# GpSimd in place of VectorE for the last decoding step of w_out, in the fused agent-attention and rational-MoE kernel

## The chip, the core and the metric

The kernel runs on one core of a Trainium2 chip. The core has five engines that run side by side and wait for each other through semaphores: TensorE (PE in the profile; its weight loads are PEld), VectorE (DVE), ScalarE (ACT), GpSimd (POOL) and SyncE (SP), which only issues DMAs here. GpSimd issues DMAs too, beside its arithmetic. The metric is the device time of one execution in microseconds (us).

## The reference

Agent attention in two stages, and after it a feed-forward layer with a rational activation. B is 2, N is 12480 tokens, the width is 128, there are 49 agents and 2048 hidden units.

```python
def sm(a, b):
    s = scale * (a @ b.transpose(0, 2, 1))
    s = s - s.max(-1, keepdims=True)
    e = np.exp(s)
    return e / (e.sum(-1, keepdims=True) + 1e-09)
agent_v = sm(agents, k) @ v
x = (sm(q, agents) @ agent_v).reshape(B * N, 128)

h = x @ w_in                                   # 24960 x 2048
P = a[0] + a[1] * h + a[2] * h**2 + a[3] * h**3
Q = 1.0 + np.abs(b[0]) * np.abs(h) + np.abs(b[1]) * h**2
out = (P / (Q + 1e-06)) @ w_out
```

w_in and w_out arrive as float64. The kernel turns them into float32 on the chip: that is the decoding of which the title speaks.

## The kernel before

The first 60 us are the setup: it makes scores and softmax of the agents over the keys of batch 0, decodes w_in, and decodes the first two of the four pieces of w_out (512 columns each, numbered 0 to 3). Then a branch on the value `flag` picks one of two main loops; with these inputs it is the fast one (`rest(True)`).

The main loop goes over 262 units. A unit is three chunks of 128 hidden units for a block of 512 tokens, so most of its tiles are 128 x 1536. For unit i:

- TensorE makes the hidden values in one of two PSUM slots (`mm1`, L495 and L496, six matmuls). It does so for unit i+1 in iteration i, and the slot is free when VectorE has finished with unit i-1.
- ScalarE squares them into the tile u (L560).
- VectorE makes the denominator part w from slot and u (L589), then the numerator part u from u and slot (L581).
- ScalarE takes logarithm and exponential of w, for two units at once (L574 and L576).
- A DMA that GpSimd issues adds a constant from the DRAM tile omd to u, for two units at once (`add_om`, L601). Before that, GpSimd builds the constant (L610), and SyncE writes it to omd (L611).
- Five iterations later GpSimd multiplies u by w (L643). Every sixteenth unit, and for the last seven, VectorE does this (L594); behind a sixteenth one GpSimd waits for it with a small copy (L646).
- Seven iterations later TensorE multiplies u by w_out into a PSUM bank (`mm2`, L503). In the first seven iterations there is nothing to multiply yet, and TensorE runs dummy matmuls (L657).

The order on each engine is the order of the program's text; no scheduler changes it. Within an iteration the calls stand as `act`, ScalarE's held work, `dve2`, `dve1`, VectorE's held work, `add_om`, L643, GpSimd's held work, and `mm1` of the next unit. "Held work" comes from three streams (queries, w_out, keys of batch 1), each of which puts a step into the lists `hold["ACT"]`, `hold["DVE"]`, `hold["POOL"]` per iteration.

Decoding a piece needs two copies on ScalarE (L177, L178), three bit operations on VectorE (L181 to L183), a multiply and an add on GpSimd (L186, L187) and at last one operation on VectorE that sets small numbers to zero (`end`, L190). In the fast loop each piece is also scaled by a factor that is known only at run time (`w_scale`, L680, on GpSimd).

Pieces 0 and 1 are decoded in the setup: the `end` of piece 0 stands behind the GpSimd steps of piece 1, and that of piece 1 is the last line of the setup. Both are scaled at the head of the main loop. Pieces 2 and 3 are decoded in the main loop by `w_stream`. Their temporaries lie in tiles of the main loop that are not in use yet: those of piece 2 in the u tiles of units 6 and 7, those of piece 3 (t, s, r, z, each 512 columns) side by side in the w tile of units 6 and 7. The `end` of piece 2 and its scaling are held for iteration 4, those of piece 3 for iteration 5. So the operation L589 of unit 6 writes over the columns in which piece 3 keeps r.

Of the kernel before, what the change touches and what calls it, by code (L numbers as in the profile page):

```python
# [16 lines left out]
ALU = mybir.AluOpType  # L17
# [28 lines left out]
TINY2 = float(np.uint32(0x38100000).view(np.float32)) ** 2  # L46
# [35 lines left out]
def agent_attention_rational_moe(  # L82
# [12 lines left out]
    PE, ACT, DVE, POOL, SP = nc.tensor, nc.scalar, nc.vector, nc.gpsimd, nc.sync  # L95
# [22 lines left out]
    wo = const.tile([128, NFC, 128], F32, name="wo")  # L118
# [15 lines left out]
    def ring(pool, n, shape, dt, nm):  # L134

        r = rings.setdefault((pool.name, nm), [[], 0])
        if len(r[0]) < n:
            r[0].append(pool.tile(shape, dt, name=f"{nm}_{len(r[0])}"))
        r[1] += 1
        return r[0][(r[1] - 1) % n]  # L140
# [26 lines left out]
    WP = DFF // 4  # L167

    def load_w(raw, src, h):
        SP.dma_start(out=raw, in_=src.bitcast(I32).rearrange("p (f w) -> p f w", w=2)[:, h * WP:(h + 1) * WP, :])  # L170

    def decode(raw, t, s, r, z, dst):

        lo, hi = raw[:, :, 0], raw[:, :, 1]

        def act():
            ACT.activation(out=r, in_=lo.bitcast(U32), func=AF.Copy, scale=2.0 ** -52)  # L177
            ACT.activation(out=z, in_=hi.bitcast(F32), func=AF.Square)  # L178

        def dve():  # L180
            DVE.tensor_scalar(out=t, in0=hi, scalar1=3, scalar2=0x3FFFFFFF, op0=ALU.logical_shift_left, op1=ALU.bitwise_and)  # L181
            DVE.scalar_tensor_tensor(out=t, in0=hi, scalar=-0x40000000, in1=t, op0=ALU.bitwise_and, op1=ALU.bitwise_or)
            DVE.tensor_scalar(out=s, in0=t, scalar1=-0x00800000, scalar2=None, op0=ALU.bitwise_and)  # L183

        def pool():
            POOL.tensor_tensor(out=r, in0=r, in1=s.bitcast(F32), op=ALU.mult)  # L186
            POOL.tensor_tensor(out=r, in0=r, in1=t.bitcast(F32), op=ALU.add)  # L187

        def end():
            DVE.scalar_tensor_tensor(out=dst, in0=z, scalar=TINY2, in1=r, op0=ALU.is_ge, op1=ALU.mult)  # L190

        return act, dve, pool, end
# [119 lines left out]
    co, arm, made = {}, {}, set()  # L312
# [365 lines left out]
    def w_scale(h):  # L678
        w = wo.rearrange("p a b -> p (a b)")[:, h * WP:(h + 1) * WP]
        POOL.tensor_scalar(out=w, in0=w, scalar1=co["Kg"], scalar2=1.0, op0=ALU.mult, op1=ALU.mult)  # L680

    def w_tiles(fast):

        u = [t[:, h].rearrange("p j t -> p (j t)") for t in rings["wk", "u"][0] for h in range(2)]
        w = [t.rearrange("p h j t -> p (h j t)") for t in rings["wk", "w"][0]]

        def part(t, i, n, dt):
            return t[:, i * WP:(i + n) * WP].bitcast(dt)

        raw = [part(t, i, 2, I32).rearrange("p (f w) -> p f w", w=2) for t, i in (((u[8], 0), (u[9], 0)) if fast else ((w[2], 0), (w[2], 2)))]  # L690
        second = [(w[3], i) for i in range(4)] if fast else [(u[8], 0), (u[8], 1), (u[9], 0), (u[9], 1)]
        tmp = [[part(t, i, 1, dt) for (t, i), dt in zip(ts, (I32, I32, F32, F32))]
               for ts in ([(u[6], 0), (u[6], 1), (u[7], 0), (u[7], 1)], second)]
        return raw, tmp

    def w_stream(fast):
        raw, tmp = w_tiles(fast)
        for h in range(2):
            load_w(raw[h], w_out, h + 2)
        decs = [decode(raw[h], *tmp[h], wo.rearrange("p a b -> p (a b)")[:, (h + 2) * WP:(h + 3) * WP]) for h in range(2)]  # L700
        for act, dve, pool, _ in decs:
            yield (None, None, [("ACT", lambda bk, f=act: f()), ("DVE", lambda bk, f=dve: f()), ("POOL", lambda bk, f=pool: f())])
        for h in range(2):
            yield (None, None, [("DVE", lambda bk, f=decs[h][3]: f())] + ([("POOL", lambda bk, h=h: w_scale(h + 2))] if fast else []))

    def a2k_stream(kv, b, G):
        ng = -(-NCK // G)
# [36 lines left out]
    with tc.manual_schedule():  # L744
# [3 lines left out]
        with tc.tile_pool(name="st", bufs=1) as sp, tc.tile_pool(name="pst", bufs=1, space=bass.MemoryType.PSUM) as pp:  # L748
# [19 lines left out]
            raws, used, pend = {}, set(), [lambda: None]  # L768
# [17 lines left out]
            def dec(kind, h):  # L786
                ts = [ring(sp, 2, [128, WP], dt, nm) for nm, dt in (("t", I32), ("s", I32), ("r", F32), ("z", F32))]
                dst = wi if kind == "i" else wo.rearrange("p a b -> p (a b)")
                *now, end = decode(raws[kind, h], *ts, dst[:, h * WP:(h + 1) * WP])
                for f in now:  # L790
                    f()
                pend.pop()()
                pend.append(end)
                used.add((kind, h))

            decs = list(DECS)

            def dec_at(when):
                while decs and decs[0][0] == when:
                    dec(*decs.pop(0)[1:])  # L800
# [4 lines left out]
            for g in range(ng):  # L805
                bk = (bank[2 * (g % 3)], bank[2 * (g % 3) + 1])
# [74 lines left out]
        def rest(fast):  # L881
            for n, d in (("q", q_t), ("pT", pT_t)):
                d.clear()
                d.update(state[n])
            for n, r in rings.items():
                r[1] = turns.get(n, 0)
            if fast:
                xb = ACT.alloc_register("xb")
                ACT.reg_load(xb, co["xb"][0:1, :].bitcast(I32))
                arm.update(om=co["om_l"], lb=co["lb_l"], xb=xb)  # L890
            else:
                arm.update(om=cab[:, 0:1], lb=c0_t)
            main(wk, [q_stream(1), w_stream(fast), a2k_stream(kv, 1, G1)], fast)
# [42 lines left out]
```

## Time and profile before

| | |
|---|---|
| median of 3 runs | 1234.26 us (1233.75 to 1234.34) |
| the profiled execution | 1236.99 us, of which the span on the core is 1235.2 us |
| PE busy | 1203.0 us, 97% of the span |
| ACT busy | 1139.0 us, 92% |
| DVE busy | 1109.9 us, 90% |
| POOL busy | 1092.1 us, 88% |
| chain that ended last | PE 63%, DVE 17%, DMA 6%, POOL 5%, issue 4%, ACT 4% |

The span runs from the first to the last instruction. A busy share is an average over stages. The chain follows the work that ended last backwards, at each step to what released it, so a piece of it is time that counts. [...] In rows of a timeline the figures in brackets are the time that the engine had been idle, and what ended it.

### The profile page before, as it was taken

Reading aid. Unit: us, or ns where it says so; the run is one execution under the profiler, and the core shown is the slowest. Engines: PE = TensorE matmul, PEld = TensorE weight load, DVE = VectorE, ACT = ScalarE, POOL = GpSimd, SP = SyncE. Lnnn points to the kernel's source line nnn. Section 1 sums busy time; section 2 is a strip of 40 time slices with the busy share of each in tenths; the row PEclk is TensorE's granted clock in tenths of the full one; section 3 lists DMA queues with packets and bytes.
Section 4 is the critical chain, followed back from the end, with each engine's and each line's share of the span. In section 5 each row is a group of like instructions: output and inputs, shape, how many; then the busy total and the mean of one; then the engine's idle time right before and its main releaser. Section 6 shows DMA issues by size and latency. Waiting matters only on the chain.

```text
span 1235.2 us, 14434 instructions
## 1 busy us (share of the span) xinstructions
PE 1203.0 (97%) x5396; PEld 706.7 (57%) x5396; DVE 1109.9 (90%) x876; ACT 1139.0 (92%) x717; POOL 1092.1 (88%) x544
## 2 busy tenths in 40 slices
PE   7979999999999999999999999999999999999998
PEld 7845555555555555555556555555555555555554
DVE  6898898988988888888989999999999998999996
ACT  3489999999999999999999999999999999999994
POOL 4549979798999989989798999999899998999993
PEclk8989999999999999999999999999999999999999
DMA  9569999898999989999899989999999989999991
GB/s 357 225 150 203 200 226 224 191 230 182 210 204 215 230 192 213 207 212 199 169 188 187 207 178 203 191 204 200 190 197 192 218 164 194 196 211 176 202 198 36
DMA packets 55312, 246.17 MB, mean 199 GB/s; under 512 B 4800, under 2 KB 5312, under 8 KB 55232
## 3 DMA queue, kind: packets, MB, share of 16 engines
q0 software_dynamic: 32768, 188.75, 79.5%
q1 hardware_dynamic: 22464, 56.39, 12.8%
q8 instruction: 45, 0.74, 0.2%
q14 instruction: 35, 0.29, 0.1%
HBM read 231.56 MB, written 13.57 MB: 198 GB/s over the span
## 4 chain that ended last, share of the span: by engine, by line
PE 63%; DVE 17%; DMA 6%; POOL 5%; issue 4%; ACT 4%; SPq 0%; DVEq 0%; ACTq 0%; POOLq 0%
PE outb L503 36%; PE slot L495 11%; PE slot L496 10%; DVE w L589 7%; DVE u L581 6%; POOL u L643 4%; DMA u<-omd 4%; ACT u L560 3%; PE outb L214 2%; DMA k<-kT 2%; PE outb L448 1%; PE outb L272 1%; ACT w L576 1%; POOL u L601 1%; DMA v<-vP 1%
## 5 line engine op out<-in xcount | busy, mean ns | idle before, releaser
L643 POOL TENSOR_TENSOR u<-u,w 128x1536 f32<-128x1536 f32 x240 | 906.4, 3985 | 14.5 <-DMA u<-omd 13.8
L503 PE MATMUL outb<-u,wo 128*128 128x512 f32 (+1 forms) x1568 | 712.9, 590 | 2.8 <-DVE av_two L278 1.3
L589 DVE SCALAR_TENSOR_TENSOR w<-slot,cf,u 128x1536 f32<-128x1536 f32 (+1 forms) x262 | 472.1, 1802 | 86.4 <-ACT u L560 66.6
L581 DVE SCALAR_TENSOR_TENSOR u<-u,cf,slot 128x1536 f32<-128x1536 f32 (+1 forms) x262 | 472.2, 1802 | 9.3
L503 PEld LDWEIGHTS outb<-u,wo 128*128 128x128 f32 x1568 | 295.3, 189 | 278.1 <-issue 242.4
L560 ACT ACTIVATE u<-slot 128x1536 f32<-128x1536 f32 (+1 forms) x262 | 380.0, 1451 | 44.1 <-PE slot L496 18.0
L495 PE MATMUL slot<-pT,m_hi 113*128 113x512 f32 (+3 forms) x800 | 370.5, 464 | 11.5 <-DVE u L581 10.5
L574 ACT ACTIVATE w<-w,cf 128x3072 f32<-128x3072 f32 (+1 forms) x134 | 374.3, 2795 | 0.5 <-DVE w L589 0.5
L576 ACT ACTIVATE w<-w 128x3072 f32<-128x3072 f32 (+1 forms) x134 | 361.9, 2703 | 0.0
L496 PE MATMUL slot<-pT,m_lo 113*128 113x512 f32 (+3 forms) x800 | 312.6, 392 | 0.0
L495 PEld LDWEIGHTS slot<-pT,m_hi 113*128 113x128 f32 x800 | 151.0, 189 | 88.2 <-DVE u L581 38.5
L601 POOL DMA_DIRECT2D u<-omd x112 | 158.5, 1415 | 31.0 <-DVE u L581 15.2
L496 PEld LDWEIGHTS slot<-pT,m_lo 113*128 113x128 f32 x800 | 151.8, 190 | 49.4 <-issue 25.3
L448 PEld LDWEIGHTS outb<-ident,p 128*113 128x113 f32 x187 | 26.2, 177 | 27.8 <-issue 14.7
L646 POOL COPY turn<-u 1x1 f32<-1x1 f32 x17 | 4.1, 241 | 41.4 <-DVE u L594 41.4
L594 DVE SCALAR_TENSOR_TENSOR u<-u,cf,w 128x1536 f32<-128x1536 f32 (+2 forms) x22 | 38.2, 1758 | 0.0
L214 PEld LDWEIGHTS outb<-ag,q 128*64 128x64 f32 x748 | 24.3, 140 | 18.1 <-issue 13.5
L448 PE MATMUL outb<-ident,p 128*113 128x128 f32 x187 | 28.7, 276 | 2.8 <-POOL p L443 2.3
L441 POOL TENSOR_TENSOR e<-e,qs 128x392 f32<-128x392 f32 (+1 forms) x25 | 29.6, 1183 | 0.1
L442 POOL TENSOR_SCALAR p<-e 128x392 fp32r<-128x392 f32 (+1 forms) x25 | 29.5, 1180 | 0.1
L214 PE MATMUL outb<-ag,q 128*64 128x49 f32 x748 | 27.3, 227 | 0.0
L186 POOL TENSOR_TENSOR r<-r,s 128x512 f32<-128x512 f32 x6 | 9.3, 1556 | 19.6 <-DVE s L183 19.6
(137 smaller groups left out, 520.1 us busy)
## 6 DMA issues: line engine op xcount, KB each, us to landing
u<-omd POOLq DMA_DIRECT2D x112, 1536.0 KB, 12.3
q<-qT SPq DMA_DIRECT2D x24, 512.0 KB, 8.6
outT<-o SPq DMA_DIRECT2D x48, 256.0 KB, 5.9
u<-omd POOLq DMA_DIRECT2D x16, 768.0 KB, 8.3
v<-vP SPq DMA_DIRECT2D x24, 258.0 KB, 8.3
k<-kT SPq DMA_DIRECT2D x24, 256.0 KB, 7.6
v<-vP SPq DMA_DIRECT2D x9, 645.0 KB, 11.4
k<-kT SPq DMA_DIRECT2D x8, 640.0 KB, 9.5
```

What stands on the lines that cost most here:

```text
L214: PE.matmul(bank[lo:hi, o:o + A], lhsT=toks[:, lo:hi], rhs=ag[:, b * A:(b + 1) * A], start=True, stop=True)
L448: PE.transpose(bank[:KR, c * CH:(c + 1) * CH], t[:, h * 4 + c, :].bitcast(F32), ident[:CH, :CH])
L495: PE.matmul(s[:, j, lo:hi], lhsT=m_hi[b][:KR, f], rhs=rhs, start=True, stop=False)
L496: PE.matmul(s[:, j, lo:hi], lhsT=m_lo[b][:KR, f], rhs=rhs, start=False, stop=True)
L503: PE.matmul(outs[blk % 2][:, :width(blk)], lhsT=wo[:, fc, :], rhs=g[:, j, :], start=fc == 0, stop=fc == NFC - 1)
L560: ACT.activation(out=x, in_=h, func=AF.Square, scale=arm["xb"], bias=1.0)
L574: ACT.activation(out=r, in_=r, func=AF.Ln, bias=arm["lb"])
L576: ACT.activation(out=r, in_=r, func=AF.Exp, scale=-1.0)
L581: DVE.scalar_tensor_tensor(out=y, in0=x, scalar=co["kap_l"], in1=h, op0=ALU.add, op1=ALU.mult)
L589: DVE.scalar_tensor_tensor(out=w, in0=h, scalar=co["mu_l"], in1=x, op0=ALU.max, op1=ALU.add)
L601: POOL.dma_start(out=t, in_=omd.unsqueeze(1).to_broadcast([128, 2, UJ * BT]), accum_op=ALU.add)
L643: POOL.tensor_tensor(out=view("u", g), in0=view("u", g), in1=view("w", g), op=ALU.mult)
```

## The change

For w_out alone, `end` becomes two operations on GpSimd: a compare with the threshold times a factor, which overwrites z, and a multiply of z by r. In the fast loop the factor for pieces 2 and 3 is that of `w_scale`, which falls away for them; for pieces 0 and 1 the factor is 1 and their scaling stays. w_in keeps the old `end`.

```diff
-    def decode(raw, t, s, r, z, dst):
+    def decode(raw, t, s, r, z, dst, on_pool=False, scale=1.0):
...
         def end():
+            if on_pool:
+                POOL.tensor_scalar(out=z, in0=z, scalar1=TINY2, scalar2=scale, op0=ALU.is_ge, op1=ALU.mult)
+                POOL.tensor_tensor(out=dst, in0=z, in1=r, op=ALU.mult)
+                return
             DVE.scalar_tensor_tensor(out=dst, in0=z, scalar=TINY2, in1=r, op0=ALU.is_ge, op1=ALU.mult)
...
-        decs = [decode(raw[h], *tmp[h], wo.rearrange("p a b -> p (a b)")[:, (h + 2) * WP:(h + 3) * WP]) for h in range(2)]
+        dst = [wo.rearrange("p a b -> p (a b)")[:, h * WP:(h + 1) * WP] for h in (2, 3)]
+        decs = [decode(raw[h], *tmp[h], dst[h], True, co["Kg"] if fast else 1.0) for h in range(2)]
...
-            yield (None, None, [("DVE", lambda bk, f=decs[h][3]: f())] + ([("POOL", lambda bk, h=h: w_scale(h + 2))] if fast else []))
+            yield (None, None, [("POOL", lambda bk, f=decs[h][3]: f())])
...
-                *now, end = decode(raws[kind, h], *ts, dst[:, h * WP:(h + 1) * WP])
+                *now, end = decode(raws[kind, h], *ts, dst[:, h * WP:(h + 1) * WP], kind == "o")
```

In the changed kernel the lines behind L170 have numbers that are 4 or 5 higher (L560 is L564 there, L589 is L593, L643 is L647), and the two new operations are L191 and L192.

On GpSimd, iterations 4 to 6 of the main loop read as follows before. The tile u_744 is that of units 0 and 1, w_752 that of units 6 and 7, and what an instruction waits for stands in brackets.

```order
L601 DMA u_745<-omd 128x2x1536
L680 TENSOR_SCALAR wo<-wo,cf 128x512 [waits DVE_49]
L643 TENSOR_TENSOR u_744<-u_744,w_749 128x1536 [waits DMASW0_49]
L441 TENSOR_TENSOR e_96<-e_96,qs_865 128x8x49
L680 TENSOR_SCALAR wo<-wo,cf 128x512 [waits DVE_49]
L601 DMA u_746<-omd 128x2x1536
```

The same place in the changed kernel, where w_754 is the tile of units 6 and 7:

```order
L605 DMA u_747<-omd 128x2x1536
L191 TENSOR_SCALAR u_749<-u_749,cf 128x512
L192 TENSOR_TENSOR wo<-u_749 128x512 [waits Pool_49]
L647 TENSOR_TENSOR u_746<-u_746,w_751 128x1536 [waits DMASW0_49]
L445 TENSOR_TENSOR e_96<-e_96,qs_867 128x8x49 [waits DVE_49]
L191 TENSOR_SCALAR w_754<-w_754,cf 128x512 [waits Activation_49]
L192 TENSOR_TENSOR wo<-w_754 128x512 [waits Pool_49]
L605 DMA u_748<-omd 128x2x1536 [waits DVE_49]
```

GpSimd no longer waits for VectorE's `end`, and has one more 128x512 multiply for each of the two pieces; the last of them stands behind the first L647 and behind a step of the queries (L445).

On VectorE, iterations 4 to 6 (units 5 and 6 at the end) before:

```order
L190 SCALAR_TENSOR_TENSOR wo<-u_747 128x512 [waits Pool_49]
L589 SCALAR_TENSOR_TENSOR w_751<-slot_721,cf,u_746 128x1536 [waits Activation_49]
L581 SCALAR_TENSOR_TENSOR u_746<-u_746,cf,slot_721 128x1536 [waits DVE_49]
L190 SCALAR_TENSOR_TENSOR wo<-w_752 128x512 [waits Pool_49]
L589 SCALAR_TENSOR_TENSOR w_752<-slot_720,cf,u_747 128x1536 [waits DVE_49,Activation_49]
```

And in the changed kernel:

```order
L438 RECIPROCAL qs_867<-qs_867 128x8 [waits DVE_49]
L593 SCALAR_TENSOR_TENSOR w_753<-slot_723,cf,u_748 128x1536 [waits Activation_49]
L585 SCALAR_TENSOR_TENSOR u_748<-u_748,cf,slot_723 128x1536 [waits DVE_49]
L593 SCALAR_TENSOR_TENSOR w_754<-slot_722,cf,u_749 128x1536 [waits Activation_49,Pool_49]
L585 SCALAR_TENSOR_TENSOR u_749<-u_749,cf,slot_722 128x1536 [waits DVE_49]
```

The two L190 are gone, and the operation that writes w of unit 6 (into w_754) now waits for GpSimd: the value that it waits for is that of the second L192 in the GpSimd rows above, which reads r from the same columns.

At the end of the setup GpSimd had, before, the last add of piece 1, the branch and the constant for omd:

```order
L187 TENSOR_TENSOR r_444<-r_444,t_442 128x512 [waits Pool_49]
L895 TENSOR_LOAD flag [waits DVE_49]
L896 COMPARE_AND_BRANCH
L610 TENSOR_SCALAR w_750<-ident,cf 128x1536 [waits DMAHW2_49,DMAHW1_49,DMAHW3_49,DMAHW0_49,DMAHW4_49,DVE_49,DMAHW5_49,PE_49,DMAHW6_49,Activation_49,DMAHW7_49,Pool_49]
L680 TENSOR_SCALAR wo<-wo,cf 128x512 x2
```

And now:

```order
L187 TENSOR_TENSOR r_444<-r_444,t_442 128x512 [waits Pool_49]
L191 TENSOR_SCALAR z_373<-z_373 128x512
L192 TENSOR_TENSOR wo<-z_373,r_372 128x512 [waits Pool_49]
L191 TENSOR_SCALAR z_445<-z_445 128x512 [waits Activation_49]
L192 TENSOR_TENSOR wo<-z_445,r_444 128x512 [waits Pool_49]
L900 TENSOR_LOAD flag [waits DVE_49]
L901 COMPARE_AND_BRANCH
L614 TENSOR_SCALAR w_752<-ident,cf 128x1536 [waits DMAHW3_49,DMAHW2_49,DMAHW4_49,DMAHW1_49,DMAHW5_49,DMAHW0_49,DMAHW6_49,PE_49,DMAHW7_49,Pool_49]
```

Four operations stand ahead of the branch. ScalarE's first square, SyncE's loads of pieces 2 and 3 with what follows them there (two loads of keys and the write of omd), and L614 itself wait for the last of the four.

## Rows read from the trace of the kernel before

**Rows 1.** Windows: us; busy (count) of PE, PEld, DVE, ACT, POOL; PEclk; DMA; GB/s.

```profile
97.00:130.00 33.00, 32.33 (x173) 18.69 (x172) 28.55 (x22) 30.52 (x21) 32.01 (x15) 1.00 0.99 210
130.00:320.00 190.00, 188.59 (x989) 109.32 (x987) 167.78 (x132) 180.59 (x124) 165.16 (x74) 1.00 0.97 211
```

**Rows 2.** The chain from 86 us on: start us, us, what.

```profile
87.14 0.56 DVE wo L190
...
91.28 1.21 DVE wo L190
...
92.58 1.83 DVE w L589
...
94.44 1.82 DVE u L581
...
96.30 0.50 PE slot L495
...
97.97 2.58 PE outb L503 x6
```

**Rows 3.** Timeline of PE: start us, us, engine, line, what [idle before, releaser].

```profile
67.31 0.50 PE L495 MATMUL slot<-pT,m_hi 113*128 113x512 f32 x1 [2.19 <-DVE u L581]
...
81.38 0.80 PE L495 MATMUL slot<-pT,m_hi 113*128 113x512 f32 x1 [2.73 <-DVE u L581]
...
84.10 2.23 PE L657 MATMUL outb<-wi,wo 128*128 128x512 f32 x4
...
91.33 0.50 PE L495 MATMUL slot<-pT,m_hi 113*128 113x512 f32 x1 [1.47 <-DVE u L581]
...
92.83 1.88 PE L657 MATMUL outb<-wi,wo 128*128 128x512 f32 x4
96.30 0.50 PE L495 MATMUL slot<-pT,m_hi 113*128 113x512 f32 x1 [1.59 <-DVE u L581]
```

**Rows 4.** Timeline of POOL, 85 to 129 us.

```profile
85.58 1.20 POOL L601 DMA_DIRECT2D u<-omd  x1
87.81 0.69 POOL L680 TENSOR_SCALAR wo<-wo,cf 128x512 f32<-128x512 f32 x1 [1.03 <-DVE wo L190]
88.47 3.45 POOL L643 TENSOR_TENSOR u<-u,w 128x1536 f32<-128x1536 f32 x1
91.90 1.28 POOL L441 TENSOR_TENSOR e<-e,qs 128x392 f32<-128x392 f32 x1
...
93.80 1.20 POOL L601 DMA_DIRECT2D u<-omd  x1
94.61 3.91 POOL L643 TENSOR_TENSOR u<-u,w 128x1536 f32<-128x1536 f32 x1
...
128.72 0.85 POOL L441 TENSOR_TENSOR e<-e,qs 128x392 f32<-128x392 f32 x1
```

**Rows 5.** Windows in which TensorE's granted clock was low; columns as in rows 1.

```profile
68.00:71.00 3.00, 3.00 (x27) 2.15 (x27) 2.80 (x2) 1.06 (x1) 0.00 (x0) 0.50 0.00 0
...
81.50:84.50 3.00, 3.00 (x7) 2.38 (x8) 2.93 (x4) 3.00 (x2) 1.43 (x2) 0.50 0.38 76
```

**Rows 6.** Line 190 for w_out in the setup: ns min/median/max, first and last start, forms.

```profile
L190 DVE SCALAR_TENSOR_TENSOR wo<-z,r x2: 684/688/692, 53.9 to 57.0; 128x512 f32<-128x512 f32 x2
```

**Rows 7.** Timeline of PE at the end of the setup.

```profile
50.14 4.18 PE L264 MATMUL bank<-v,S 128*49 128x129 f32 x36
```

**Rows 8.** Timeline of POOL, 55 to 72 us.

```profile
55.75 1.26 POOL L187 TENSOR_TENSOR r<-r,t 128x512 f32<-128x512 f32 x1
58.17 1.55 POOL L610 TENSOR_SCALAR w<-ident,cf 128x1536 f32<-128x1536 f32 x1 [1.16 <-PE outb L301]
...
71.15 1.40 POOL L601 DMA_DIRECT2D u<-omd  x1 [10.09 <-DVE u L581]
```

**Rows 9.** Timeline of ACT at the head of the main loop.

```profile
62.10 2.79 ACT L560 ACTIVATE u<-slot 128x1536 f32<-128x1536 f32 x2 [0.78 <-PE slot L496]
```

**Rows 10.** DMA issues: out<-in, engine, count, KB, us to landing.

```profile
omd<-w SPq DMA_DIRECT2D x1, 768.0 KB, 7.8
```

## The prediction, as it was made before the run

> **What bounds the kernel now.** I read the windows by stage first. From 97 us on TensorE is busy nearly all the time: 32.33 of 33 us, and then 188.59 of 190 us at full clock [rows 1]. So the kernel is bound by TensorE once the main loop runs full, and a time by which its work starts later is not given back there. The stage that the change touches lies before it. There I read the chain of waits and the timelines side by side. The chain from 87 to 96.3 us is VectorE without a break, and both removed operations stand on it: piece 2's `end` with 0.56 us, piece 3's with 1.21 us, then w and u of unit 6 with 1.83 and 1.82 us, and at 96.30 us TensorE, which from there on is the chain itself [rows 2]. TensorE's timeline says the same from the other side: its first matmul of units 7 and 8 came after 1.47 and 1.59 us of idle time that VectorE's u ended [rows 3]. Whatever VectorE loses or gains there reaches TensorE in full.
>
> **The change part by part.**
>
> *VectorE, main loop.* The two operations go. Taken alone, that is 0.56 + 1.21 = 1.8 us of the chain. Piece 2's share comes through: w and u of unit 5 start 0.56 us earlier, and so does TensorE's unit 7 (90.8 in place of 91.33). Piece 3's does not, for the operation that writes w of unit 6 now waits for GpSimd's last multiply of piece 3, which reads r from the same columns. Behind it on VectorE stand its own u and all later units, and TensorE's unit 8 waits for that u. So the question is when this multiply ends, against the 92.58 us at which w of unit 6 began before.
>
> *GpSimd, iterations 4 and 5.* I start from the DMA issue at 85.58 us, ahead of which nothing changes. The next operation can begin 0.81 us after such an issue, as 93.80 and 94.61 show [rows 4]: 86.39. The compare of piece 2 is a tensor_scalar of 128x512 as the scaling was, 0.69 us [rows 4]: 87.08. Its multiply is a tensor_tensor of 128x512; the add of L187 in that shape took 1.26 us [rows 8]: 88.34. That is as early as L643 began before (88.47), since the wait of 1.03 us for VectorE's `end` is gone [rows 4]. L643 took 3.43 us to the start of the next [rows 4]: 91.77. The query step L441 took 1.28 us there and 0.85 us at 128.72 [rows 4]. The long one ran beside piece 3's L190 on VectorE (chain, 91.28 to 92.49 [rows 2]), which itself took 1.21 us against 0.56 us for piece 2's, while GpSimd waited. Both operations were slow together, and one of them is gone, so I take 0.85: 92.62. Compare and multiply of piece 3, 0.69 + 1.26: 94.57. Three times an operation waits for the one before it by semaphore (multiply for compare, twice, and VectorE for the multiply); from L190's end (87.70 [rows 2]) to L680's start (87.81 [rows 4]) such a step took 0.11 us, so 0.33 in all: 94.9. Then w of unit 6 begins 2.3 us later than at 92.58, and u of unit 6 and TensorE's unit 8 with it, at 98.6 in place of 96.30.
>
> [...]
>
> What no row shows is a compare on GpSimd. Bounds from both sides: no shorter than the scaling, 0.69 us, since it moves the same bytes, and at most what the two-input multiply costs, 1.26 us. I take 0.69, the row with the same shape and the same kind of instruction, and keep for the range 2 x 0.57 = 1.1 us more. With L441 at 1.28 as well the delay would be 3.9 us in place of 2.3; without the hand-overs 2.0.
>
> *TensorE's clock.* TensorE finishes its dummy matmuls of iteration 6 at 92.83 + 1.88 - 0.56 = 94.15 us [rows 2, 3] and then has nothing until 98.6: 4.4 us idle. [...] What it costs, from the case at 81.38 us: the six matmuls took until 84.10, 2.72 us, against 96.30 to 97.97, 1.67 us, at full clock, and the dummies behind took 2.23 against 1.88 us [rows 2, 3]: 1.05 + 0.35 = 1.4 us. At 81.38 VectorE was the limit and hid it; behind 96.30 TensorE itself is the chain, so here it counts. At most 1.7 us is lost, half of the 3.4 us or so for which the low clock lasted.
>
> *GpSimd and its followers later.* Its DMA issue of 93.80 comes at 94.9, and L643 of unit 1 with it, 1.1 us later than before; TensorE's need moves by 3.7 us, so GpSimd gains room. Cost nothing.
>
> *The setup.* VectorE's first L190, 0.68 us [rows 6], stood on the way to the normalisation, but that waits for TensorE's matmuls, which end at 54.32 [rows 7], 0.2 us before it: between 0 and 0.2 us gained, taken as 0. The second lay beside other waits: 0. GpSimd's four operations follow L187, which ends at 57.01 [rows 8]: 2 x (0.69 + 1.26) + 2 x 0.11 = 4.1 us, so to 61.1. ScalarE's first square waits for that, and began at 62.10, after TensorE [rows 9]: hidden with 1.0 us to spare. SyncE's loads and the constant for omd move from 58.17 to 61.2, 3.0 us; the write of omd, issued at the constant's end (62.8) and 7.8 us under way [rows 10], lands at 70.6. Its first reader, the DMA issue of 71.15, waited for VectorE until then [rows 8]: hidden with 0.5 us to spare. Should the compares be long, this cover is gone, and 0.6 us of the 1.1 us would show there.
>
> **The sum.** 2.3 + 1.4 + 0 = 3.7 us. The profiled execution took 1236.99 us (1235.2 and 1.8 around it), so 1240.7 for its like; it stood 2.7 us above the median of 1234.26, so the time is 1234.26 + 3.7 = 1238.0 us.
>
> **The rivals.**
>
> *The wait without the clock.* If TensorE keeps its full clock, 2.3 us remain: 1236.6. For it: its idle times of 1.47 and 1.59 us cost nothing, and two falls are few to judge by. Against it: 2.19 us were enough for one of them.
>
> *The delay is swallowed but for GpSimd's.* If the loop is carried by GpSimd and its DMAs, the end moves by the 1.1 us of these: 1235.4. For it: from 97 to 130 us GpSimd is busy 32.01 of 33 us and the DMAs 0.99. Against it: TensorE has hardly an idle moment there, and from 130 to 320 GpSimd is idle for 25 of 190 us [rows 1].
>
> *The compare is slow.* At the price of the multiply: 1.1 us more in the loop, perhaps 0.4 for L441: 1239.1 to 1239.5. Against it: nothing in the rows has such a price for a one-input operation. [...]
>
> *Faster.* VectorE gets its 1.8 us and nothing waits: 1232.5. The mechanism is that GpSimd ends the multiply of piece 3 before VectorE comes to unit 6, at 92.58 - 1.8 = 90.8 us; from there on the change gains. GpSimd would have to be 4 us quicker than its rows over a path of 9 us. For it only that the order of the work has L643 in that path, 3.43 us, and that even without it 0.7 us would be lacking.
>
> **How the numbers follow.** A measurement of this kernel can tell about 0.2%, 2.5 us, from no change. Forecast 0.58, with 1236.5 to 1239 as its own range; wait without the clock 0.15; GpSimd's delay alone 0.12; slow compare 0.10; faster 0.05. The range of 1235.0 to 1239.9 takes in the bounds of the compare and the two smaller delays and leaves out the gain. Slower by over 0.2% (above 1236.7): 0.56 of the forecast, the slow compare, and 0.02 of the wait alone, 0.68. Within 0.2%: 0.02 + 0.13 + 0.11 = 0.26. Faster: 0.06.
>
> **What would show it.** In the changed profile: VectorE's w of unit 6 behind 3.5 to 5.5 us of idle time, ended by GpSimd's L192; L192 itself at about 1.3 us and L191 at 0.7; TensorE's unit 8 behind 4 us or more of idle time and a granted clock of 0.50 for some 3 us after it; the first L643 no later than before; in the setup no idle time of ScalarE or VectorE ended by GpSimd. The prediction is wrong if VectorE's w of unit 6 begins before 93 us, if L192 of piece 3 ends ahead of it without a wait, or if TensorE's unit 8 starts 3.7 us late in work done and the end does not move.

## The result and the profile after

The changed kernel is slower: 1245.63 us (median of 5 runs, 1243.95 to 1248.02) against 1234.03 (1233.37 to 1234.34). The ratio is 1.0088 with a 95% interval of 1.0076 to 1.0100, which is 9.4 to 12.3 us. Forecast were 1238.0 us and a range of 1235.0 to 1239.9. The direction was right; 3.7 us more were forecast, and the measured change is three times that.

GpSimd's timeline of the changed kernel (start us, us, engine, line, what, idle before and its releaser), first in the setup, then in the loop. [rows 8] and [rows 4] show the same stretches before:

```profile
55.45 1.26 POOL L187 TENSOR_TENSOR r<-r,t 128x512 f32<-128x512 f32 x1
56.78 1.97 POOL L191 TENSOR_SCALAR z<-z 128x512 f32<-128x512 f32 x1
58.84 1.27 POOL L192 TENSOR_TENSOR wo<-z,r 128x512 f32<-128x512 f32 x1
60.19 1.92 POOL L191 TENSOR_SCALAR z<-z 128x512 f32<-128x512 f32 x1
62.20 1.28 POOL L192 TENSOR_TENSOR wo<-z,r 128x512 f32<-128x512 f32 x1
63.66 1.54 POOL L614 TENSOR_SCALAR w<-ident,cf 128x1536 f32<-128x1536 f32 x1 [0.18 <-POOL wo L192]
...
73.70 1.41 POOL L605 DMA_DIRECT2D u<-omd  x1 [7.17 <-DMA omd<-w]
...
87.33 1.20 POOL L605 DMA_DIRECT2D u<-omd  x1
88.63 1.99 POOL L191 TENSOR_SCALAR u<-u,cf 128x512 f32<-128x512 f32 x1
90.70 1.28 POOL L192 TENSOR_TENSOR wo<-u 128x512 f32<-128x512 f32 x1
91.94 3.48 POOL L647 TENSOR_TENSOR u<-u,w 128x1536 f32<-128x1536 f32 x1
95.40 0.83 POOL L445 TENSOR_TENSOR e<-e,qs 128x392 f32<-128x392 f32 x1
96.34 2.00 POOL L191 TENSOR_SCALAR w<-w,cf 128x512 f32<-128x512 f32 x1
98.42 1.27 POOL L192 TENSOR_TENSOR wo<-w 128x512 f32<-128x512 f32 x1
```

All four L191 take 1.92 to 2.00 us, where the scaling, a tensor_scalar of the same shape, took 0.69 [rows 4]. The multiplies (1.27 to 1.28), L647 (3.48) and L445 (0.83) take what was forecast. Three things follow. First, in the setup the last L192 ends at 63.48, and ScalarE's first square now waits for it; the first DMA of the loop (above, at 73.70) waits for the write of omd. ScalarE's timeline:

```profile
63.51 2.79 ACT L564 ACTIVATE u<-slot 128x1536 f32<-128x1536 f32 x2 [2.49 <-POOL wo L192]
```

Before, this square was released by TensorE [rows 9]. Second, VectorE waits twice: its w of unit 2 for the write of omd, whose source lies in that very tile, and its w of unit 6 for the last L192 (VectorE's timeline, w of units 2 and 6):

```profile
73.24 1.82 DVE L593 SCALAR_TENSOR_TENSOR w<-slot,cf,u 128x1536 f32<-128x1536 f32 x1 [1.00 <-DMA omd<-w]
...
99.72 1.82 DVE L593 SCALAR_TENSOR_TENSOR w<-slot,cf,u 128x1536 f32<-128x1536 f32 x1 [7.29 <-POOL wo L192]
```

Third, TensorE, idle for 7.57 us, makes unit 8 and the first `mm2` at the low clock (its timeline; then a window with busy us of PE, PEld, DVE, ACT, POOL, PEclk, which is TensorE's granted clock as a share of its full speed, DMA share, GB/s):

```profile
103.44 0.79 PE L499 MATMUL slot<-pT,m_hi 113*128 113x512 f32 x1 [7.57 <-DVE u L585]
104.03 0.63 PE L500 MATMUL slot<-pT,m_lo 113*128 113x512 f32 x1
...
106.16 4.54 PE L507 MATMUL outb<-u,wo 128*128 128x512 f32 x6
110.54 0.60 PE L452 MATMUL outb<-ident,p 128*113 128x128 f32 x4
```

```profile
103.50:109.00 5.50, 5.50 (x10) 3.37 (x11) 4.54 (x3) 2.60 (x2) 5.42 (x4) 0.50 1.05 213
```

The clock was 0.50 for all of those 5.5 us of work. Before, the same work began at 96.30 and ran at full clock. Its first `mm2` in the timeline of TensorE:

```profile
97.81 2.74 PE L503 MATMUL outb<-u,wo 128*128 128x512 f32 x6
```

From the first matmul to the first `mm2` it was 1.51 us there and 2.72 here, and the six of `mm2` took 2.74 there and 4.54 here: 1.21 + 1.80 = 3.0 us.

Where the time went shows in VectorE's w, unit by unit. The setup itself ends at another time in each execution (first matmul of m at 56.39 in after and at 58.43 in e2, with the same setup), so the table counts from the first matmul of m (L301, or L305; 56.69 us in before, 56.39 in after) to the start of w, and gives the difference to before in us. Before's own values are 6.90, 14.79, 35.89, 43.05 and 56.99 us. Behind unit 11 the differences stay the same for many units (in after 10.45 at unit 25, 10.25 at unit 60).

| kernel | first matmul of m at | unit 0 | unit 2 | unit 6 | unit 8 | unit 11 | time against before, 95% interval |
|---|---|---|---|---|---|---|---|
| after | 56.39 | +1.70 | +2.06 | +7.44 | +8.45 | +10.45 | 1.0076 to 1.0100 |
| e1 loop only | 57.30 | -0.01 | -0.73 | +4.67 | +5.68 | +7.39 | 1.0051 to 1.0081 |
| e2 setup only | 58.43 | +1.70 | +2.22 | +2.22 | +2.22 | +2.21 | 1.0018 to 1.0038 |
| e3 minimum | 55.58 | +1.69 | +2.01 | +7.40 | +8.41 | +8.92 | 1.0095 to 1.0149 |
| e4 warm | 56.37 | +1.71 | +1.97 | +7.35 | +7.35 | +7.35 | 1.0054 to 1.0083 |
| e5 apart | 55.77 | +1.71 | +2.18 | +0.18 | +1.90 | +7.81 | 1.0043 to 1.0072 |
| e6 apart, loop only | 57.17 | -0.01 | -0.74 | -2.74 | -1.01 | +4.67 | 1.0039 to 1.0068 |
| e10 later | 57.86 | -0.01 | -0.74 | -2.13 | +1.03 | +0.20 | 0.9992 to 1.0020 |
| e11 no compare | 57.15 | -0.02 | -0.74 | +1.90 | +2.91 | +4.81 | 1.0033 to 1.0077 |
| e12 no compare, apart | 56.93 | -0.02 | -0.70 | -2.69 | -1.95 | +1.84 | 1.0004 to 1.0034 |

The 10.45 us of after are 2.06 at unit 2 (setup), 5.38 more at unit 6 (the wait), and 3.01 more behind it. The -0.7 at unit 2 in some kernels goes with the clock of 0.50 that TensorE had from 68 to 71 us in the profiled execution of before [rows 5], where theirs was higher (over the same 3 us 1.00 in e11 and 0.79 in e1). Against an execution of before without it, the setup's share and the whole would be an estimated 0.7 us more. The spans of the two profiled executions differ by 8.0 us only: from unit 210 to unit 220 the difference falls from 10.50 to 8.38 us, and that of e2 as well, from 1.37 to -0.88, so it is the execution of before that lost time there. Its TensorE waited 1.86 us for GpSimd at 1041.87 us (its timeline):

```profile
1041.87 0.69 PE L448 MATMUL outb<-ident,p 128*113 128x128 f32 x4 [1.86 <-POOL p L443]
```

### The profile page after: what moved, and what is told of

It reads as the page before. It is cut to its first block, busy times and chain, and to the rows that moved or that the text cites. A ratio compares the mean times of both kernels' runs of the same rounds, so it can differ in the third digit from the quotient of the medians.

```text
span 1243.2 us, 14432 instructions
## 1 busy us (share of the span) xinstructions
PE 1204.6 (97%) x5396; PEld 706.5 (57%) x5396; DVE 1104.9 (89%) x872; ACT 1138.6 (92%) x717; POOL 1103.9 (89%) x550
## 3 DMA queue, kind: packets, MB, share of 16 engines
q1 hardware_dynamic: 22464, 56.39, 12.7%
## 4 chain that ended last, share of the span: by engine, by line
PE 67%; DVE 19%; ACT 5%; issue 3%; POOL 3%; DMA 2%; SPq 0%; DVEq 0%; POOLq 0%; ACTq 0%
PE outb L507 39%; PE slot L499 12%; PE slot L500 11%; DVE w L593 8%; DVE u L585 7%; ACT u L564 3%; PE outb L218 2%; PE outb L452 2%; ACT w L580 1%; DMA k<-kT 1%; PE outb L276 1%; POOL u L647 1%; DMA v<-vP 1%; DMA omd<-w 1%; DVE t L182 1%
## 5 line engine op out<-in xcount | busy, mean ns | idle before, releaser
L647 POOL TENSOR_TENSOR u<-u,w 128x1536 f32<-128x1536 f32 x240 | 906.1, 4025 | 7.3 <-DMA u<-omd 7.1
L507 PE MATMUL outb<-u,wo 128*128 128x512 f32 (+1 forms) x1568 | 714.4, 591 | 2.8 <-DVE av_two L282 1.4
L593 DVE SCALAR_TENSOR_TENSOR w<-slot,cf,u 128x1536 f32<-128x1536 f32 (+1 forms) x262 | 471.9, 1801 | 97.0 <-ACT u L564 71.8
L507 PEld LDWEIGHTS outb<-u,wo 128*128 128x128 f32 x1568 | 296.2, 189 | 278.8 <-issue 244.2
L564 ACT ACTIVATE u<-slot 128x1536 f32<-128x1536 f32 (+1 forms) x262 | 379.8, 1450 | 52.4 <-PE slot L500 28.6
L452 PEld LDWEIGHTS outb<-ident,p 128*113 128x113 f32 x187 | 26.3, 177 | 25.2 <-issue 16.2
L445 POOL TENSOR_TENSOR e<-e,qs 128x392 f32<-128x392 f32 (+1 forms) x25 | 30.9, 1236 | 0.1
L452 PE MATMUL outb<-ident,p 128*113 128x128 f32 x187 | 28.6, 275 | 0.4
L447 POOL TENSOR_TENSOR p<-e,p 128x392 fp32r<-128x392 f32 (+1 forms) x25 | 25.0, 1001 | 2.1
```

Source lines behind the costliest of these rows:

```text
L452: PE.transpose(bank[:KR, c * CH:(c + 1) * CH], t[:, h * 4 + c, :].bitcast(F32), ident[:CH, :CH])
L507: PE.matmul(outs[blk % 2][:, :width(blk)], lhsT=wo[:, fc, :], rhs=g[:, j, :], start=fc == 0, stop=fc == NFC - 1)
L564: ACT.activation(out=x, in_=h, func=AF.Square, scale=arm["xb"], bias=1.0)
L593: DVE.scalar_tensor_tensor(out=w, in0=h, scalar=co["mu_l"], in1=x, op0=ALU.max, op1=ALU.add)
L647: POOL.tensor_tensor(out=view("u", g), in0=view("u", g), in1=view("w", g), op=ALU.mult)
```

## The experiments

The theory after the result: three losses that add up (setup 2.1, wait 5.4, low clock 3.0 us), all of them from the compare that takes 2.0 us. Rivals: the setup's delay or the clock's share is hidden by the others; L191 is slow by its place and not by what it computes; behind the wait GpSimd's lateness counts, not the clock.

**e1, only the loop's pieces on GpSimd.**

```diff
-                *now, end = decode(raws[kind, h], *ts, dst[:, h * WP:(h + 1) * WP], kind == "o")
+                *now, end = decode(raws[kind, h], *ts, dst[:, h * WP:(h + 1) * WP], False)
```

> Only the two pieces of the main loop end on GpSimd; the two of the setup end on VectorE as before. Theory (three losses that add up: 1.8 us in the setup, 5.4 us by which VectorE's w of unit 6 waits for GpSimd in the loop, 3.0 us of TensorE's low clock behind that wait): the first square starts at 62.1 again, w of units 0 to 4 as before, w of unit 6 about 5.4 us later than before, time 1243 to 1244.5. Rival (the setup's delay is hidden by the longer wait in the loop): 1245.5, as with all four pieces on GpSimd.

Measured: 1242.46 us. From unit 2 to unit 6 it loses 5.40 us, as after does (5.38), and to unit 11 it is 3.1 us less late than after. The wait is not shortened by an earlier setup; the setup's share adds. The time lies 0.5 us below the expected 1243 to 1244.5.

**e2, only the setup's pieces on GpSimd.**

```diff
-        decs = [decode(raw[h], *tmp[h], dst[h], True, co["Kg"] if fast else 1.0) for h in range(2)]
+        decs = [decode(raw[h], *tmp[h], dst[h]) for h in range(2)]
...
-            yield (None, None, [("POOL", lambda bk, f=decs[h][3]: f())])
+            yield (None, None, [("DVE", lambda bk, f=decs[h][3]: f())] + ([("POOL", lambda bk, h=h: w_scale(h + 2))] if fast else []))
```

> Only the two pieces of the setup end on GpSimd; the two of the main loop end on VectorE as before. Theory: the first square waits for GpSimd (63.5 in place of 62.1), the write of omd lands at 73.2, w of unit 2 begins 1.8 us late and all later units with it, no wait of VectorE for GpSimd at unit 6; time 1235.5 to 1236.5. Rival (the setup's delay is given back before unit 8, since the loop's first units wait for each other anyway): 1234.0.

Measured: 1237.48 us, 2.2 to 4.7 us above before and 1.0 us above the expected range; w of unit 2 is 2.2 us late, and unit 11 as much. Nothing of it is given back. What the two operations taken from VectorE in the setup were worth, 0 in the prediction, isn't shown: the table counts from behind the first of them.

**e4, TensorE kept at work during the wait.**

```diff
-                for _ in range(DUM):
+                for _ in range(DUM + 7 * (i == 6)):
```

> The changed kernel with seven more dummy matmuls (6.6 us) on TensorE in iteration 6, in the 7.6 us in which it waits for unit 8. Theory (behind the wait TensorE ran at the low clock, and lost 3.0 us by it): granted clock 1.00 behind 103.4, w of unit 6 still at 99.7, w of unit 11 at 130.8 - 3.0 - 10.2 + 10.2 = about 7.2 us late in place of 10.2; time 1242 to 1243.5. Rival (what is lost behind unit 8 is GpSimd's lateness, not the clock): unit 11 still 10 us late, 1245.5.

Measured: 1242.48 us. The timeline and the window of TensorE:

```profile
93.88 7.89 PE L661 MATMUL outb<-wi,wo 128*128 128x512 f32 x18
...
104.83 2.74 PE L507 MATMUL outb<-u,wo 128*128 128x512 f32 x6
```

```profile
103.50:109.00 5.50, 5.50 (x21) 3.57 (x22) 5.43 (x4) 3.97 (x2) 5.42 (x4) 1.00 1.05 214
```

With dummies in the gap the clock stays at 1.00, L507's six take 2.74 us in place of 4.54, and the delay stays at 7.35 us from unit 6 to 11. So the 3.0 us behind unit 6 are the low clock. In time it gave back 3.2 us of after's median (the intervals of the two ratios overlap a little, 1.0054 to 1.0083 and 1.0076 to 1.0100; the times themselves don't).

**e3, a minimum in place of the compare**, to see whether the compare is what is slow.

```diff
-                POOL.tensor_scalar(out=z, in0=z, scalar1=TINY2, scalar2=scale, op0=ALU.is_ge, op1=ALU.mult)
+                POOL.tensor_scalar(out=z, in0=z, scalar1=TINY2, scalar2=scale, op0=ALU.min, op1=ALU.mult)
```

(with the factor divided by the threshold)

> All four pieces on GpSimd, but the compare is replaced by a minimum with the threshold (and the factor by factor / threshold, one more 128x1 operation in the setup), so that the same bytes go through the same kind of instruction without a compare. Theory (the compare itself is slow, 2.0 us for 128x512 in place of 0.69): L191 takes 0.7 us, the setup hides it all, VectorE waits about 4.2 us at unit 6, w of unit 6 is 2.3 us late, and with the low clock behind it the time is 1237 to 1239, the sum of the prediction. Rival (a tensor_scalar in this place is slow whatever it computes, by its place, its operands or VectorE beside it): L191 stays at 2.0 us and the time at 1245.5.

Measured: the theory fell. L191 took 1.92 to 2.00 us as in after, VectorE waited 7.3 us, and the time was 1247.15 us (1243.89 to 1255.79). It is not the compare as such.

This run shows one thing more. The delay at unit 6 is that of after, but behind it only 1.5 us are lost by unit 11, in place of 3.0. TensorE's timeline and window:

```profile
102.59 0.80 PE L500 MATMUL slot<-pT,m_hi 113*128 113x512 f32 x1 [7.56 <-DVE u L586]
...
105.31 3.03 PE L508 MATMUL outb<-u,wo 128*128 128x512 f32 x6
```

```profile
103.50:109.00 5.50, 5.50 (x17) 3.38 (x17) 4.50 (x4) 3.45 (x2) 5.42 (x4) 0.78 1.00 204
```

The idle time is the same as in after (7.56 and 7.57 us), and it is 2.72 us to the first `mm2` here too, but the clock was back during `mm2`, whose six took 3.03 us in place of 4.54. So the same idle time cost 3.0 us in one execution and 1.5 in another (2.7 in that of e1).

**e9, four kinds of operation in one kernel**, one execution, read for its durations alone.

```diff
-                POOL.tensor_scalar(out=z, in0=z, scalar1=TINY2, scalar2=scale, op0=ALU.is_ge, op1=ALU.mult)
+                POOL.tensor_scalar(out=z, in0=z, **scale)
...
+    forms = (dict(scalar1=TINY2, scalar2=1.0, op0=ALU.mult, op1=ALU.mult), dict(scalar1=TINY2, scalar2=None, op0=ALU.is_ge),
+             dict(scalar1=1.0, scalar2=TINY2, op0=ALU.mult, op1=ALU.is_ge), dict(scalar1=TINY2, scalar2=1.0, op0=ALU.subtract, op1=ALU.mult))
```

> The changed kernel with another pair of operations in each of its four L191, so what it computes is not the reference's; only the durations are read. Piece 0: multiply, multiply with constants (the pair of the scaling). Piece 1: the compare alone. Piece 2: multiply, then compare. Piece 3: subtract, multiply. Theory (GpSimd has a quick form for multiply and add only, and takes 2 us for others): 0.7 us for piece 0, about 2 us for pieces 1 and 2, 0.7 or 2 us for piece 3. First rival (what is slow is the place or the operand, z as ScalarE left it): 2 us for piece 0 as well. Second rival (two different operations in one instruction are slow): 0.7 us for pieces 0 and 1, 2 us for 2 and 3.

GpSimd's timeline, the operation of pieces 0 to 3 (L194 there):

```profile
57.80 0.62 POOL L194 TENSOR_SCALAR z<-z 128x512 f32<-128x512 f32 x1
...
59.85 1.53 POOL L194 TENSOR_SCALAR z<-z 128x512 f32<-128x512 f32 x1
...
88.01 1.94 POOL L194 TENSOR_SCALAR u<-u 128x512 f32<-128x512 f32 x1
...
95.62 1.95 POOL L194 TENSOR_SCALAR w<-w 128x512 f32<-128x512 f32 x1
```

Multiply with multiply takes 0.62 us in the same place, on the same operand, as the 1.97 of after. A compare alone takes 1.53, multiply with compare 1.94, subtract with multiply 1.95. So the place is excluded, and so is "two different operations". What is quick here is the pair of multiplies; a compare and a subtract are slow, as the minimum was in e3. Why they are slow no run shows.

**e5, the wait of VectorE taken away**, by other places for r and z of piece 3.

```diff
-        second = [(w[3], i) for i in range(4)] if fast else [(u[8], 0), (u[8], 1), (u[9], 0), (u[9], 1)]
+        second = [(w[3], 0), (w[3], 1), (u[8], 2), (u[9], 2)] if fast else [(u[8], 0), (u[8], 1), (u[9], 0), (u[9], 1)]
```

> The changed kernel with r and z of piece 3 in the unused last third of the u tiles of units 8 and 9, in place of the w tile of units 6 and 7: GpSimd's work and its order stay as they are, but VectorE's w of unit 6 no longer waits for its last multiply. Theory (the wait at unit 6 is what lets GpSimd's lateness reach the end): VectorE goes straight on to unit 6, no idle time of 7 us and no low clock at unit 8; ScalarE's square of unit 8 waits some 1.5 us for GpSimd instead, TensorE waits 1 to 2 us for L647 of unit 1; time 1236 to 1238.5, so 7 to 9 us less than the changed kernel. Rival (GpSimd's own lateness, about 6 us at its next DMA issue, sets the end): 1240 or more.

Measured: 1242.28 us; the rival is right. Unit 6 is on time (+0.18), but unit 11 is 7.81 us late. TensorE's timeline shows the new wait:

```profile
105.43 1.20 PE L452 MATMUL outb<-ident,p 128*113 128x128 f32 x4 [5.57 <-POOL p L447]
```

The transposes of the queries stand in TensorE's order of iteration 7 and wait for GpSimd's L447, which stands behind both pieces and L647 of unit 1. So GpSimd's added work reaches TensorE by a second way, which the wait at unit 6 had covered. Behind this wait too TensorE ran at the low clock for a while (0.50 from 103.5 to 106.5 us; the four of L452 take 1.20 us, where the four of L448 took 0.60 at 100.38 us in before), and the four take 1.20 us behind the like waits of e6 and e12.

**e6, as e5, with the setup's pieces on VectorE** (the edits of e1 and e5 together).

> As the run before it, and the two pieces of the setup end on VectorE again. Theory: the setup's 2.1 us and the wait's 5.3 and the clock's 3.0 us are all gone; VectorE is 1.8 us earlier at unit 6, GpSimd 4 us later at its next DMA issue, TensorE waits about 2 us for L647 of units 1 and 2: 1234 to 1236. Rival (GpSimd's lateness counts in full): 1238.

Measured: 1241.75 us; the rival's mechanism again, and almost 4 us more than the time that it gave. Unit 6 comes 2.74 us early, unit 11 4.67 us late:

```profile
103.95 1.20 PE L452 MATMUL outb<-ident,p 128*113 128x128 f32 x4 [5.68 <-POOL p L447]
```

**e10, the kernel before with piece 3's `end` one iteration later on VectorE**, with the places of e5.

```diff
+            if fast and h:
+                yield (None, None, [])
             yield (None, None, [("DVE", lambda bk, f=decs[h][3]: f())] + ([("POOL", lambda bk, h=h: w_scale(h + 2))] if fast else []))
```

> The kernel before, all four ends on VectorE, with r and z of piece 3 in the last third of the u tiles of units 8 and 9, and piece 3's end and scaling one iteration later (behind u of unit 6). Theory (only what stands ahead of u of unit 6 on VectorE is on the chain, since TensorE is the limit from unit 8 on): TensorE's unit 8 comes 1.2 us earlier, 1233.0. Rival (what is gained ahead of unit 8 is lost again, for ScalarE is busy without a break there): 1234.2, no change.

Measured: 1235.75 us, a ratio of 0.9992 to 1.0020: no change, and no version that beats before. That is the rival's outcome, but not by its reason: unit 6 is 2.13 us early and unit 7 is 1.03 us late, for the moved operation met L643 on GpSimd (VectorE's timeline, then GpSimd's):

```profile
95.20 3.25 DVE L190 SCALAR_TENSOR_TENSOR wo<-u 128x512 f32<-128x512 f32 x1
```

```profile
93.92 3.90 POOL L643 TENSOR_TENSOR u<-u,w 128x1536 f32<-128x1536 f32 x1
```

The same operation took 0.64 us for piece 2 in this execution. TensorE's clock in it bears on the prediction (its timeline, then a window):

```profile
68.47 0.50 PE L495 MATMUL slot<-pT,m_hi 113*128 113x512 f32 x1 [2.19 <-DVE u L581]
...
81.80 0.50 PE L495 MATMUL slot<-pT,m_hi 113*128 113x512 f32 x1 [2.73 <-DVE u L581]
```

```profile
83.00:86.00 3.00, 2.18 (x6) 0.78 (x5) 2.96 (x3) 3.00 (x2) 2.51 (x3) 1.00 0.00 0
```

The idle time of 2.73 us, which preceded the low clock in before [rows 3], is followed by 1.00 here. Behind that of 2.19 us, which preceded it too, w of unit 2 begins 0.74 us earlier than in before; by this the clock was, in an estimate, higher there as well.

**e11, the compare left out**: the prediction's own case, a quick L191.

```diff
-                POOL.tensor_scalar(out=z, in0=z, scalar1=TINY2, scalar2=scale, op0=ALU.is_ge, op1=ALU.mult)
+                POOL.tensor_scalar(out=z, in0=z, scalar1=0.0, scalar2=scale, op0=ALU.mult, op1=ALU.add)
```

> The changed kernel with the compare left out: L191 is z times 0 plus the factor (multiply, add), so small numbers are not set to zero. Theory (the prediction's mechanism was right and only the size of L191 was off): L191 takes 0.65 to 0.7 us, no wait for GpSimd in the setup, VectorE waits 4 to 4.5 us at unit 6, unit 6 is 2.3 us late, and with a low clock behind it unit 11 is 3.7 to 4.3 us late, time 1237.5 to 1239. Rival (the delay of unit 6 is given back as GpSimd and the DMAs have time meanwhile): 1235 or less.

Measured: 1240.36 us, 4.1 to 9.5 us above before. GpSimd's, VectorE's and TensorE's timelines:

```profile
85.30 1.21 POOL L605 DMA_DIRECT2D u<-omd  x1
86.11 1.15 POOL L191 TENSOR_SCALAR u<-u,cf 128x512 f32<-128x512 f32 x1
...
92.86 0.69 POOL L191 TENSOR_SCALAR w<-w,cf 128x512 f32<-128x512 f32 x1
93.64 1.27 POOL L192 TENSOR_TENSOR wo<-w 128x512 f32<-128x512 f32 x1
```

```profile
94.94 1.82 DVE L593 SCALAR_TENSOR_TENSOR w<-slot,cf,u 128x1536 f32<-128x1536 f32 x1 [4.56 <-POOL wo L192]
```

```profile
98.66 0.79 PE L499 MATMUL slot<-pT,m_hi 113*128 113x512 f32 x1 [4.84 <-DVE u L585]
...
101.39 4.44 PE L507 MATMUL outb<-u,wo 128*128 128x512 f32 x6
```

The setup is hidden again (unit 0: -0.02), and VectorE waits 4.56 us; from unit 2 to unit 6 it loses 1.90 + 0.74 = 2.6 us. Three of the four L191 take 0.62 to 0.69 us; the one directly behind the DMA issue takes 1.15. The clock then takes 2.9 us more to unit 11, twice what was predicted. The theory holds for the wait and the setup. The time is above its 1237.5 to 1239: the delay at unit 11 is 0.5 us more than it gave, by the clock, and the rest lies within the interval.

**e12, the compare left out and the places of e5** (both edits together).

> As the run before it (compare left out), and r and z of piece 3 in the last third of the u tiles of units 8 and 9, so that VectorE doesn't wait at unit 6. First theory (VectorE's two operations are worth their 1.8 us once nothing waits for GpSimd; the prediction's last rival): 1232.5. Second theory (GpSimd is as late as its own added work, and the transposes of the queries, L452, wait for its L447, which before ended 0.3 us ahead of them): unit 8 comes early, then L452 waits 2 to 3 us, unit 11 is 1.0 to 2.5 us late, 1235.2 to 1236.8.

Measured: 1236.89 us, 0.5 to 4.2 us above before. The second theory is right, with the time at the upper end of its range: unit 8 is 1.95 us early, then TensorE waits for GpSimd, and unit 11 is 1.84 us late.

```profile
100.95 1.20 PE L452 MATMUL outb<-ident,p 128*113 128x128 f32 x4 [2.82 <-POOL p L447]
```

## Why the prediction was wrong

**The step that failed** is "The compare of piece 2 is a tensor_scalar of 128x512 as the scaling was, 0.69 us", together with its upper bound, "at most what the two-input multiply costs, 1.26 us". It measured 1.99 us, outside the bounds. The kind of instruction and the shape were those of [rows 4], the operations in it were not, and with the place and the operand of piece 0 the same these alone made 1.97 us (after) or 0.62 (e9). No row of before has such an operation at this size, and a bound from the two-input multiply was no bound. This step alone doesn't carry the miss: with a quick L191 the median was still 1240.36 us (e11), just above the range, because other terms of the sum were too small as well.

The terms of the sum, one by one:

- *The wait at unit 6*, forecast 2.3 us, measured 5.4. The mechanism was right to the instruction: VectorE's w of unit 6, GpSimd's second L192, idle time of TensorE behind it. The difference is 2 x 1.3 us for the compares, and 0.5 us because L191 began 1.30 us after the DMA issue (87.33 to 88.63) where 0.81 was taken from a multiply. A quick L191 there ended late as well: it began after 0.81 us but took 1.15 in place of 0.69 (e11), and L192, which waits for its end, began late by that. The prediction's own rows show the like, L643 at 3.91 us directly behind an issue and at 3.45 elsewhere [rows 4]. With a quick L191 the term came out at 2.6 (e11).
- *The setup*, forecast 0, measured 2.1 (e2). GpSimd's four operations took 6.7 us from 56.78 to 63.48, not 4.1. The prediction said that the cover would go if compares were long and priced it at 0.6 us; the compares were longer than its bound, and both covers that it named, 1.0 us at the first square and 0.5 us at the write of omd, were used up. It also took the DMA issue for the first to wait for that write; VectorE's w of unit 2 waited for it ahead of the issue (73.24 against 73.70).
- *The clock*, forecast 1.4 us, measured 3.0 (e4). That it would fall was right; but the length of the idle time doesn't tell: the 2.73 us behind which it fell to 0.50 in before left it at 1.00 in e10. In all runs with 4.8 us or more of idle time ahead of unit 8 it did fall (to 0.50 in after, e1 and e11; 0.78 on the mean of 103.5 to 109 us in e3). The price came from the one case at 81.38, a part of which was the dummies behind unit 5's matmuls, 0.35 us. In after `mm2` lost 1.8 us in their place, with 4.84 us idle in e11 1.7, and with 7.56 us idle in e3 only 0.3. So how long the low clock lasts changes from one execution to the next, the bound "at most 1.7 us" fell, and 1.5 us, near the forecast, occurs as well. A smaller slip: the 1.67 us at full clock are from the chain and the 2.72 at the low clock from a timeline; by timelines alone the six matmuls cost 1.2 us more, not 1.05.
- *GpSimd and its followers later: "Cost nothing"*. Wrong as a statement on its own, though after could not show it: L452 waits for L447 (5.57 us in e5, 2.82 in e12). In before L443 ended at 100.07 and L448 began at 100.38, 0.3 us of room, which the prediction left out.

**The rivals.** The slow compare had a tenth of the chances, and was right in kind, at 0.57 us more a compare where 1.3 were measured. "Faster" fails even without the wait that it asked to be gone: in e12 nothing waits at unit 6, and TensorE then waits for GpSimd's L447. "The wait without the clock" and "GpSimd's delay alone" didn't come about. The short L445 was right: 0.83 us with L190 gone.

**The sum.** 2.1 + 5.4 + 3.0 = 10.5 us, against 9.4 to 12.3 by the runs. The three are steps of one row of the table, so that they add up to its 10.45 shows nothing by itself; that each is a loss of its own is shown by e1 and e2 for the setup, by e11 for a part of the wait, and by e4 for the clock.

## What to carry to other kernels

Take a duration on GpSimd over from another instruction only if the operations in it are the same, not just its kind and shape: a tensor_scalar of 128x512 took from 0.62 to 2.03 us here by its operations (e9, e6). Otherwise the unshown operation needs a far wider upper bound, and a cover of half a microsecond is none. When a wait is found, ask who else waits for the late engine: its added work can arrive by a second path that the first one hides, so that taking the first wait away gives back little (e5). The idle time that was added ahead of TensorE's full load cost more than itself here, and one case doesn't give the price of the low clock: the same 7.6 us of idle time cost 1.5, 2.7 and 3.0 us more (e3, e1, after), so it needs a range.

## What the runs showed of the hardware

- GpSimd's tensor_scalar on 128x512 float32: 0.62 to 0.69 us for multiply with multiply or multiply with add where no DMA issue stands directly ahead (before, e9, e11, e12), 1.53 for one compare (e9), 1.92 to 2.03 for a compare, a minimum or a subtract paired with a multiply (after, e3, e6, e9).
- The operation directly behind a DMA issue of GpSimd ended about 0.5 us later than its usual start and duration give: a quick tensor_scalar took 1.15 us in place of 0.69 (e11), a slow one began 1.30 us after the issue in place of 0.81 (after), and L643 took 3.91 us in place of 3.45 (before).
- VectorE's L190 took 0.64 to 0.69 us beside no GpSimd work (before, e10), 0.68 in the setup with its last 0.45 us beside L186 (before), 1.28 beside L441 (before) and 3.25 beside L643 (e10). What sets it apart no run shows.
- With seven more dummy matmuls in a wait of 7.6 us TensorE's clock was 1.00 behind it, in place of 0.50, which was worth 3 us (e4, after).
- The same idle time of TensorE can be followed by either clock, and the low clock lasts differently long: 2.73 us were followed by 0.50 in before and by 1.00 in e10, and behind 7.6 us `mm2` took 4.54 us in after and 3.03 in e3.
